# Weight strips and residual tiles moved as 120 + 8 partitions instead of eight row groups

## The chip, the cores and the metric

The kernel runs on one core of one Trainium2 chip. The metric is device time in microseconds from the start of the program to its end; lower is better. Before the change the median of three runs is 2310.73 us (2308.09 to 2316.26).

## The reference

The input x has 2048 tokens of 576 features. Two kinds of layer alternate, A, B, A, B, each with a residual and a layer norm in front.

```python
x = x + A(layernorm(x), wqkv, wo)          # same weights in both A layers
x = x + B(layernorm(x), mem0, Wq, Wk, Wv, Wo)
x = x + A(layernorm(x), wqkv, wo)
x = x + B(layernorm(x), mem0, Wq, Wk, Wv, Wo)

def A(x):      # 32 heads of 18, window of 8 keys at distances 0, 2, .. 14
    q, k, v = split(x @ wqkv)               # wqkv: 576 x 1728
    attn = softmax(q . k[s - 2w] * scale)   # w = 0..7, masked below 0
    return (attn . v[s - 2w]) @ wo          # wo: 576 x 576

def B(x):      # 32 heads of 128, segments of 32 tokens, 8 memory rows
    mem = mem0
    for s in range(64):
        h = concat(mem, x[32 * s : 32 * s + 32])
        o = attention(h @ Wq, h @ Wk, h @ Wv, mask) @ Wo
        mem = o[:8]                         # goes into the next segment
        out[s] = o[8:]
```

B is a recurrence: a segment's memory comes out of the segment before it.

## The kernel before

Everything is held transposed, features on partitions: 576 features are five blocks of up to 128 partitions. B's weights stay in on-chip memory for the whole run. A's weights do not fit beside them and are streamed.

The four layers run at the same time. Step t of the main loop (`b_step`) handles segment t of the first B layer (lane 0) and segment t-5 of the second (lane 1) in one set of matmuls, so there are 69 steps. An A tile has 64 tokens (`T`); there are 32 tiles in each A layer, and `a_tile(1, j)` runs ahead of lane 0, `a_tile(3, j)` between lane 0 and lane 1. One step of B has a pass for q and k (L834, L837), one for v (L881), scores (L921 to L931), the product with v (L972) and the output projection (L996). An A tile has its q, k and v projections (L572), logits (L621), the spreading of the softmax weights (L646) and its output projection (L682).

What sets the order: the kernel builds a list of operations with an engine, an estimated duration, a priority, dependencies and buffers. A planner in the program (`_Plan.run`) plays this list through at build time and emits the instructions in the order in which its own clock starts them. Each engine then executes its instructions in that fixed order. SP issues nearly all DMAs, also in order; a DMA that has to wait holds up those behind it.

A's weights are cut into 12 strips: three for each of q, k and v, and three for the output projection. A strip has 256 columns (128 for the third one of q, k and v, and of the output projection), five row blocks side by side: 1280 (or 640) bfloat16 numbers on each of 128 partitions, 320 KB or 160 KB. `wload` brings one strip for one A tile:

- the first use gathers it from the weight in HBM into a piece of `wo`'s buffer (L505, L506);
- the second and third use (`COPY = 2`) gather it into one of three `ring` buffers; after the third, L515 writes it to a copy of its own in HBM, `strips[i]`, laid out as the buffer is;
- every later use fetches this copy into a ring buffer (L509). That is 732 fetches: 488 of 320 KB and 244 of 160 KB.

A fetch into a ring buffer waits until TensorE has read the strip that was there (three strips earlier), and until that strip's own DMA had landed.

The residual of a tile, `xT` (128 x 5 x 64 float32, 160 KB), is written to `x1T` or `x3T` in HBM once A's output is added (L691), and read back by `residual` for the B lane that adds to it (L717): 32 times each for two layers, 128 transfers.

All these HBM copies have one shape. The 128 rows of a buffer lie in eight groups (`NQU`) of 16 (`RQU`), each group followed by one unused row, so that the groups are not contiguous and the outermost dimension of a transfer is 8:

```python
self.x1T = dp.tile([NQU, P // NQU + 1, NT, 5, T], F32, name="x1T")
self.strips = [dp.tile([NQU, P // NQU + 1, 5 * 256], BF16, name=f"strip{i}") for i in range(12)]
dma(out=w.t[:, 0:5 * n], in_=self.strips[i][:, 0:RQU, 0:5 * n])
```

Of the kernel before, what the change touches and what calls it, by code (L numbers as in the profile page):

```python
# [8 lines left out]
F32 = mybir.dt.float32  # L9
BF16 = mybir.dt.bfloat16  # L10
# [6 lines left out]
P = 128  # L17
# [10 lines left out]
T = 64  # L28
# [7 lines left out]
EPS = 1e-5  # L36
NQ = T // 16
CB = (0, 126, 252, 378, 448)
NQU = 8
RQU = P // NQU  # L40


class _Buf:
# [206 lines left out]
class _K:  # L250
# [37 lines left out]
    def setup(self):  # L288
        nc, tc = self.nc, self.tc
# [2 lines left out]
                                                           act_func_set_id=6, ins=[], outs=[]))  # L292
        dp = self.pool("dram", 1, space=bass.MemoryType.DRAM)
        NT = self.NT
        self.x1T = dp.tile([NQU, P // NQU + 1, NT, 5, T], F32, name="x1T")
        self.x3T = dp.tile([NQU, P // NQU + 1, NT, 5, T], F32, name="x3T")
        self.strips = [dp.tile([NQU, P // NQU + 1, 5 * 256], BF16, name=f"strip{i}") for i in range(12)]
        self.pre()

        self.ident = ident = cp.tile([P, P], BF16, name="ident")  # L300
# [190 lines left out]
    def wload(self, i, src, rows, col0, n, prio, dep):  # L491

        pl, dma = self.pl, self.nc.sync.dma_start
        step, last = rows
        self.strip_n[i] = k = self.strip_n.get(i, -1) + 1
        w = pl.buf("ring") if k else None

        def view():  # L500
            return (w.t if k else self.wo[:, i * 1280:(i + 1) * 1280])[:, 0:5 * n].rearrange("p (k n) -> p k n", k=5)

        def gather(e):
            f, v, r, m = src[0:1, col0:col0 + 1], view(), min(P, src.shape[0] - last), min(n, src.shape[1] - col0)
            dma(out=v[:, 0:4, 0:m], in_=bass.AP(f.tensor, f.offset, [[src.shape[1], P], [step * src.shape[1], 4], [1, m]]))  # L505
            (dma if k else self.nc.scalar.dma_start)(out=v[0:r, 4, 0:m], in_=src[last:last + r, col0:col0 + m])  # L506

        def fetch(e):
            dma(out=w.t[:, 0:5 * n], in_=self.strips[i][:, 0:RQU, 0:5 * n])  # L509
        if k == 0:  # L510
            o = self.first = pl.op("SP", 0.65, gather, -20.0 + 0.01 * i, lat=4.0)
            return view, (), o
        o = pl.op("SP", 0.9 if k <= COPY else 0.5, gather if k <= COPY else fetch, prio, [dep, self.strip_in.get(i)], acq=[w], lat=4.0)
        if k == COPY:
            self.strip_in[i] = pl.op("SP", 0.5, lambda e: dma(out=self.strips[i][:, 0:RQU, 0:5 * n], in_=w.t[:, 0:5 * n]), prio, [o], uses=[w])  # L515
        return view, (w,), o

    def a_tile(self, layer, j, dep, due, span):

        nc, pl = self.nc, self.pl  # L520
# [3 lines left out]
        def pr(f):  # L524
            return due - span * (1.0 - f)
        Q = PR[f"A{layer}"]
        if layer == 1:
            xT = pl.buf("x1")
# [8 lines left out]
            b = pl.op("PE", 0.16, tr, pr(0.04), [a], acq=[ps, xT], uses=[x0], mm=5)  # L537
            o_x = pl.op(AD_, _evac(320), lambda e, ps=ps: self.copy(e, xT.t[:], ps.t[:, 0:5 * T].rearrange("p (c t) -> p c t", c=5)),
                        pr(0.05), [b], uses=[ps, xT])
        else:  # L540
            xT = self.acc[0][j][0]
# [19 lines left out]
        for part in (0, 1, 2):  # L561
            ps = pl.buf("r")
            o = o_n
            for c in range(5):
                if c % 2 == 0:
                    n = 256 if c < 4 else P
                    view, w, ow = self.wload(part * 3 + c // 2, self.A_wqkv, (P, 512), part * D + CB[c], n, pr(Q[1]) - PR[f"ring{layer}"], wgate)
                w0 = c % 2 * CB[1]

                def mm(e, c=c, view=view, ps=ps, w0=w0):  # L570
                    for kc in range(5):
                        nc.tensor.matmul(ps.t[:, c * T:(c + 1) * T], lhsT=view()[:, kc, w0:w0 + P], rhs=xn.t[:, kc, :],  # L572
                                         start=(kc == 0), stop=(kc == 4))
                o = pl.op("PE", 0.146, mm, pr(Q[1] + 0.03 * part), [o, ow], acq=[ps, dst[part]] if c == 0 else (),
                          uses=[xn, *w] if c == 0 else [xn, *w, ps], lat=0.0 if c < 4 else None, mm=5)
                if c == 0 and part > 0:
                    def hcopy(e, part=part):
# [3 lines left out]
                        else:  # L581
                            self.copy(e, h, hin[0].t[:, part - 1])
                    got[part, "h"] = pl.op("DVE" if first else ("POOL", "ACT") if early else "POOL", 0.25, hcopy, pr(Q[1]), [o] if first else [o, hin[1]],
                                           uses=[dst[part]] if first else [dst[part], hin[0]])
# [22 lines left out]
        o = None  # L607
        for n, (c0, nb) in enumerate(((0, 2), (2, 2), (4, 1))):
            def prod(e, c0=c0, nb=nb):
                self.tt(e, big.t[:, c0:c0 + nb], qT.t[:, c0:c0 + nb].unsqueeze(2).to_broadcast([P, nb, AW, T]),  # L610
                        win(kT.t, c0, nb), ALU.mult)
            o = pl.op(("POOL", "DVE") if early else "POOL", (1.0 * nb + 0.05, 0.15 + 0.3 * nb), prod, pr(Q[2] + 0.02 * n), [o] if o else [got[0], got[1], got[1, "h"]],
                      acq=[big] if n == 0 else (), uses=[qT, kT] if n == 0 else [big, qT, kT], lk=True)
# [9 lines left out]
        o = o_l = pl.op("PE", 0.29, logits, pr(Q[3]), [o], acq=[psL, e_], uses=[big], mode="C", mm=20)  # L623

        def amax(e):
            v = psL.t[:, 0:P].rearrange("p (w t) -> p w t", w=AW)
            if first:
# [3 lines left out]
        o = pl.op("DVE", 0.6, amax, pr(Q[3]), [o], acq=[nmx], uses=[psL])  # L631
        o = pl.op("ACT", 0.28, lambda e: nc.scalar.activation(out=e_.t[:], in_=psL.t[:, 0:P].rearrange("p (w t) -> p w t", w=AW),
                                                              func=ACT.Exp), pr(Q[3]), [o], uses=[psL, e_])

        def norm(e):
            nc.vector.tensor_reduce(out=ssum.t[:], in_=e_.t[:].rearrange("p w t -> p t w"), axis=AX.X, op=ALU.add)
            nc.vector.reciprocal(out=ssum.t[:], in_=ssum.t[:])
        o = pl.op("DVE", 0.68, norm, pr(Q[3]), [o], acq=[ssum], uses=[e_])
        o = pl.op("DVE", 0.3, lambda e: self.tt(e, e_.t[:], e_.t[:], ssum.t[:].unsqueeze(1).to_broadcast([P, AW, 16]), ALU.mult),
                  pr(Q[3]), [o], uses=[e_, ssum], lk=True)  # L640

        def spread(ps, c0, nb):
            for c in range(nb):
                for g in range(NQ):
                    q4 = slice(g * AH, (g + 1) * AH)
                    nc.tensor.matmul(ps[g].t[:, c * P:(c + 1) * P], lhsT=self.epadT[q4, c0 + c, :],  # L646
                                     rhs=e_.t[q4].rearrange("p w t -> p (w t)"), start=True, stop=True, skip_group_check=True)
        b = o
        evs = {}
        for n, (c0, nb) in enumerate(((0, 2), (2, 3))):  # L650
            ps = [pl.buf("r") for _ in range(NQ)]
            b = pl.op("PE", 0.03 + 0.05 * nb, lambda e, ps=ps, c0=c0, nb=nb: spread(ps, c0, nb), pr(Q[4] + 0.02 * n), [b], acq=ps,
                      uses=[e_], mode="R", mm=4 * nb)
# [6 lines left out]
        for c0, nb in ((0, 2), (2, 2), (4, 1)):  # L660
# [6 lines left out]
        o = pl.op(PD, (2.6, 0.85), lambda e: self.tt(e, big.t[:, :, 0:4], big.t[:, :, 0:4], big.t[:, :, 4:8], ALU.add),  # L667
                  pr(Q[5] + 0.02), mus, uses=[big], lk=True)
        o = pl.op(PD, (1.44, 0.5), lambda e: self.tt(e, big.t[:, :, 0:2], big.t[:, :, 0:2], big.t[:, :, 2:4], ALU.add),
                  pr(Q[5] + 0.04), [o], uses=[big], lk=True)  # L670
        o = o_o = pl.op(PD, (0.78, 0.33), lambda e: self.tt(e, oT.t[:], big.t[:, :, 0], big.t[:, :, 1], ALU.add),
                        pr(Q[5] + 0.06), [o], acq=[oT], uses=[big], lk=True)
        ps = pl.buf("r")
        for mb in range(5):
            if mb % 2 == 0:
                n = 256 if mb < 4 else P
                view, w, ow = self.wload(9 + mb // 2, self.A_wo, (CB[1], CB[4]), mb * P, n, pr(Q[6]) - PR[f"ring{layer}"], o_l)
            w0 = mb % 2 * P

            def mm(e, mb=mb, view=view, ps=ps, w0=w0):  # L680
                for c in range(5):
                    nc.tensor.matmul(ps.t[:, mb * T:(mb + 1) * T], lhsT=view()[:, c, w0:w0 + P], rhs=oT.t[:, c, :], start=(c == 0), stop=(c == 4))  # L682
            o = pl.op("PE", 0.147, mm, pr(Q[6]), [o, ow], acq=[ps] if mb == 0 else (),
                      uses=[oT, *w] if mb == 0 else [oT, *w, ps], lat=0.0 if mb < 4 else None, mm=5)
        if layer == 1 and first:
            for d in self.wo_in:
                pl.after(d, o)
        o = pl.op("DVE", 0.49, lambda e: nc.vector.tensor_tensor(out=xT.t[:], in0=xT.t[:],
                                                                 in1=ps.t[:, 0:5 * T].rearrange("p (c t) -> p c t", c=5), op=ALU.add),
                  pr(Q[6]), [o], uses=[ps, xT])  # L690
        xst = pl.op("SP", 0.5, lambda e: nc.sync.dma_start(out=(self.x1T if layer == 1 else self.x3T)[:, 0:RQU, j], in_=xT.t[:]),  # L691
                    pr(0.95), [o], uses=[xT])
        (self.x1_stored if layer == 1 else self.x3_stored)[j] = xst
        xnb = pl.buf(f"xnb{layer}")
# [1 line left out]
        def wr2(e, m, rstd):  # L696
# [5 lines left out]
            for o, i, bc in views:  # L702
                self.tt(e, o, i, bc(m), ALU.subtract)
                self.tt(e, o, o, bc(rstd), ALU.mult)
        o = self.layernorm(xT, o, pr(Q[7]), wr2, 2.5, wacq=[xnb], early=early)
        o = pl.op("ACT", 0.27, lambda e: self.copy(e, xnb.t[64:128, :, 5, :], xnb.t[0:64, :, 4, :]),
                  pr(Q[7]), [o], uses=[xnb])
# [3 lines left out]
    def residual(self, lane, j, dep, prio):  # L711

        nc, pl = self.nc, self.pl
        b = pl.buf(("x3", "x5")[lane])
        xb = pl.buf("fin") if lane == 1 else None
        src = (self.x1T, self.x3T)[lane]
        o = pl.op("SP", 0.5, lambda e: nc.sync.dma_start(out=b.t[:], in_=src[:, 0:RQU, j]), prio,  # L717
                  [dep, (self.x1_stored, self.x3_stored)[lane][j]], acq=[b] if xb is None else [b, xb])
        self.acc[lane][j] = (b, o, xb)

# [443 lines left out]
```

## Time and profile before

| | |
|---|---|
| median of three runs | 2310.73 us |
| profiled execution: device time | 2308.09 us |
| profiled execution: span of the trace | 2306.4 us |
| mean granted TensorE clock | 0.977 |
| ring<-strip, L509 | 732 issues, median 574 ns each on SP |
| strip<-ring, L515 | 12 issues, median 622 ns |
| x1T<-x and x3T<-x, L691 | 64 issues, median 597 and 608 ns |
| x<-x1T and x<-x3T, L717 | 64 issues, median 575 and 574 ns |
| all DMA instructions on SP | 997 |
| DMA traffic | 265.12 MB, mean 115 GB/s |
| queue q1 (transfers issued by SP) | 145040 packets, 237.35 MB, 32.4% of 16 engines' span |
| queue q8 (instructions) | 474 packets, 7.77 MB, 1.4% of 16 engines' span |

How to read it. The span is cut by engine; PE is TensorE's matmul row and PEld its weight-load row, both fed by one sequencer. SPq is SP's queue: there, time is spent in issuing a DMA and in waiting for what it needs, and the transfer itself runs on the 16 DMA engines. "a <- b" in a table of waits means that a stood idle until b was done. "issue" is idle time for which the profile shows no wait. In lines of the stretches ("windows") the numbers after the engines' busy times are the granted clock, the mean busy share of the 16 DMA engines, and GB/s. The prediction below shows the lines of the page that it uses.

### The profile page before, as it was taken

What the parts mean: (1) busy time and instruction counts of PE and PEld (TensorE: products, weight loads), DVE (VectorE), ACT (ScalarE), POOL (GpSimd) and SP (SyncE); (2) the same over time, 40 slices, a digit from 0 to 9 for tenths busy, and PEclk for the clock granted to TensorE, in tenths of its full rate; (3) what the DMA queues carried; (4) which work ended last, traced back from release to release, by engine and by line L of the source; (5) the groups of instructions that cost most, each with busy time, mean ns of one, the idle gap of its engine ahead of it and who ended that gap; (6) DMA issues with size and microseconds to landing.
All of it is one profiled execution on the core that took longest, in us unless ns stands there. A gap on an engine that the chain in (4) does not pass through costs nothing.

```text
span 2306.4 us, 132983 instructions
## 1 busy us (share of the span) xinstructions
PE 2068.6 (90%) x60717; PEld 1754.8 (76%) x60717; DVE 1421.1 (62%) x3754; ACT 1140.4 (49%) x2803; POOL 834.1 (36%) x1289
## 2 busy tenths in 40 slices
PE   2788899999999999999999999899899899999988
PEld 1566787788778877887787888778788777877876
DVE  4466666666566666666666666566666566665565
ACT  1343544555455544555555555455455455555544
POOL 3234334433333443343344433333443333442221
PEclk7798999999999999999999999999999999999999
DMA  9643333333333333333333333333433333332220
GB/s 317 181 132 121 100 108 121 114 112 113 114 111 111 117 122 104 115 119 118 107 108 131 113 112 106 114 110 109 127 113 113 103 117 117 108 118 70 70 68 12
DMA packets 151331, 265.12 MB, mean 115 GB/s; under 512 B 16488, under 2 KB 82928, under 8 KB 150640
## 3 DMA queue, kind: packets, MB, share of 16 engines
q1 hardware_dynamic: 145040, 237.35, 32.4%
q0 software_dynamic: 4576, 18.88, 2.4%
q8 instruction: 474, 7.77, 1.4%
q14 instruction: 89, 0.73, 0.1%
q10 hardware_dynamic: 1152, 0.39, 0.1%
HBM read 240.46 MB, written 16.12 MB: 111 GB/s over the span
## 4 chain that ended last, share of the span: by engine, by line
PE 59%; DMA 36%; issue 2%; DVE 1%; SPq 1%; ACT 0%; ACTq 0%; DVEq 0%
DMA ring<-strip 33%; PE r L834 19%; PE r L996 15%; PE r L881 7%; PE r L837 4%; PE r L572 4%; PE r L682 2%; PE r L972 2%; PE r L646 1%; DMA x<-in_B_mem_dram 1%; PE r L931 1%; PE r L472 1%; PE r L921 1%; DMA ring<-in_A_wqkv_dram 1%; PE r L621 1%
## 5 line engine op out<-in xcount | busy, mean ns | idle before, releaser
L834 PE MATMUL r<-hT,wq 128*128 128x80 bf16 (+1 forms) x8832 | 664.4, 199 | 6.2 <-issue 2.9
L834 PE MATMUL r<-hT,wk 128*128 128x80 bf16 (+1 forms) x8832 | 665.6, 199 | 1.9 <-issue 1.9
L834 PEld LDWEIGHTS <-wq 128*128 128x128 bf16 x8832 | 504.5, 99 | 49.4 <-issue 36.9
L837 PE MATMUL r<-hT,wqk_r 128*128 128x160 bf16 (+1 forms) x2208 | 509.1, 231 | 0.0
L278 ACT ACTIVATE qk<-r 128x480 bf16<-128x480 f32 (+2 forms) x668 | 351.0, 526 | 276.8 <-PE r L837 265.7
L834 PEld LDWEIGHTS <-wk 128*128 128x128 bf16 x8832 | 449.8, 100 | 3.4 <-issue 3.3
L996 PE MATMUL r<-OT,wo 128*128 128x80 bf16 (+1 forms) x11040 | 419.7, 201 | 26.1 <-issue 21.8
L996 PEld LDWEIGHTS <-wo 128*128 128x128 bf16 x11040 | 397.8, 100 | 36.0 <-issue 32.1
L881 PE MATMUL r<-wv,hT 128*32 128x512 bf16 x5376 | 360.4, 385 | 1.5 <-issue 1.2
L285 POOL TENSOR_TENSOR big<-qT,kT 128x1024 bf16<-128x1024 bf16 x189 | 314.5, 1684 | 122.1 <-ACT kT L278 83.3
L285 POOL TENSOR_TENSOR ex<-ex,sum 128x320 bf16<-128x320 bf16 x138 | 107.1, 776 | 580.1 <-DVE sum L781 540.8
L572 PE MATMUL r<-xn,ring 128*128 128x64 bf16 x4725 | 207.9, 195 | 107.0 <-DMA ring<-strip 83.9
L572 PEld LDWEIGHTS <-ring 128*128 128x128 bf16 x4725 | 167.8, 99 | 147.7 <-DMA ring<-strip 109.1
L881 PEld LDWEIGHTS <-hT 128*32 128x32 bf16 x6720 | 172.4, 97 | 132.1 <-issue 9.7
L278 ACT ACTIVATE V<-r 128x512 bf16<-128x512 f32 x305 | 181.6, 596 | 181.2 <-PE r L881 181.0
L770 DVE TENSOR_REDUCE nmx<-r 128x8 f32<-128x320 f32 x276 | 133.4, 483 | 160.7 <-PE r L925 160.0
L837 PEld LDWEIGHTS <-wqk_r 128*128 128x128 bf16 x2208 | 220.6, 100 | 0.0
L278 ACT ACTIVATE OT<-r 128x320 bf16<-128x320 f32 (+1 forms) x378 | 134.4, 422 | 159.0 <-PE r L972 158.0
L278 ACT ACTIVATE big<-r 128x256 bf16<-128x256 f32 (+1 forms) x288 | 109.3, 430 | 88.7 <-PE r L646 87.9
L285 POOL TENSOR_TENSOR xnb<-x,st 128x256 bf16<-128x256 f32 x124 | 64.5, 520 | 235.9 <-DVE st L478 235.9
L771 DVE TENSOR_TENSOR r<-r,nmx 128x320 f32<-128x320 f32 x276 | 137.8, 499 | 9.5
L1015 DVE CAST hT<-r 128x64 bf16<-128x64 f32 (+1 forms) x68 | 14.9, 220 | 197.2 <-PE r L996 197.1
(147 smaller groups left out, 2989.8 us busy)
## 6 DMA issues: line engine op xcount, KB each, us to landing
ring<-strip SPq DMA_DIRECT2D x488, 320.0 KB
ring<-strip SPq DMA_DIRECT2D x244, 160.0 KB
x1T<-x SPq DMA_DIRECT2D x32, 160.0 KB
x<-x1T SPq DMA_DIRECT2D x32, 160.0 KB
x3T<-x SPq DMA_DIRECT2D x32, 160.0 KB
x<-x3T SPq DMA_DIRECT2D x32, 160.0 KB
wo<-in_B_Wo_dram POOLq DMA_DIRECT2D x4, 1152.0 KB, 25.3
wq<-in_B_Wq_dram POOLq DMA_DIRECT2D x2, 2048.0 KB, 21.2
```

Of the source, the lines that this page charges most:

```text
L278: nc.scalar.activation(out=out, in_=in_, func=ACT.Copy, scale=1.0 if scale is None else scale)
L285: (self.nc.vector if e == "DVE" else self.nc.gpsimd).tensor_tensor(out=out, in0=in0, in1=in1, op=op)
L472: nc.tensor.matmul(psf, lhsT=(self.ones if c < 4 else self.ones_h)[:, :], rhs=xs.t[:, c].rearrange("p a t -> p (a t)"), start=(c == 0), st ...
L572: nc.tensor.matmul(ps.t[:, c * T:(c + 1) * T], lhsT=view()[:, kc, w0:w0 + P], rhs=xn.t[:, kc, :], start=(kc == 0), stop=(kc == 4))
L682: nc.tensor.matmul(ps.t[:, mb * T:(mb + 1) * T], lhsT=view()[:, c, w0:w0 + P], rhs=oT.t[:, c, :], start=(c == 0), stop=(c == 4))
L770: nc.vector.tensor_reduce(out=m, in_=v, axis=AX.X, op=ALU.max, negate=True)
L771: nc.vector.tensor_tensor(out=v, in0=v, in1=m.unsqueeze(len(shp) - 1).to_broadcast(shp), op=ALU.add)
L834: nc.tensor.matmul(pv[:, hh, wi, a:b], lhsT=self.Wb[wi][0][:, kc, h * P:(h + 1) * P], rhs=hT.t[:, kc, a:b], start=(hh == 0 and wi == 0 and ...
L837: nc.tensor.matmul(pv[:, hh, :, a:b], lhsT=self.Wb[0][1][:, h * P:(h + 1) * P], rhs=hT.t[:, 4:6, a:b], start=False, stop=(hh == n - 1), sk ...
L881: nc.tensor.matmul(ps.t[c * 32:(c + 1) * 32, :], lhsT=l, rhs=w, start=(kc == 0), stop=(kc == 4))
L972: nc.tensor.matmul(ps[c].t[:, i * n + a - c0:i * n + z - c0], lhsT=V[b].t[q4, r, i, :], rhs=pt.t[q4, i, b, a:z], start=(i == 0 and b == bl ...
L996: nc.tensor.matmul(psY.t[:, mb * W80 + c0:mb * W80 + c1], lhsT=self.wo[:, w0:w0 + P], rhs=self.OT[:, h % 16 // 4 * 8 + h // 16 * 4 + h % 4 ...
```

## The change

The HBM copies lose their groups and unused rows: they are plain tensors of 128 rows. Each transfer to or from them is issued as two DMAs, one for partitions 0 to 119 and one for partitions 120 to 127. The planner's costs, dependencies, buffers and priorities are as before: both DMAs belong to one planned operation, so they stand next to each other in SP's order, and the instruction that uses the data waits for both.

```diff
-NQU = 8
-RQU = P // NQU
+PQU = (slice(0, 120), slice(120, 128))
...
-        self.x1T = dp.tile([NQU, P // NQU + 1, NT, 5, T], F32, name="x1T")
-        self.x3T = dp.tile([NQU, P // NQU + 1, NT, 5, T], F32, name="x3T")
-        self.strips = [dp.tile([NQU, P // NQU + 1, 5 * 256], BF16, name=f"strip{i}") for i in range(12)]
+        self.x1T = dp.tile([P, NT, 5, T], F32, name="x1T")
+        self.x3T = dp.tile([P, NT, 5, T], F32, name="x3T")
+        self.strips = [dp.tile([P, 5 * 256], BF16, name=f"strip{i}") for i in range(12)]
...
         def fetch(e):
-            dma(out=w.t[:, 0:5 * n], in_=self.strips[i][:, 0:RQU, 0:5 * n])
+            for p in PQU:
+                dma(out=w.t[p, 0:5 * n], in_=self.strips[i][p, 0:5 * n])
...
         if k == COPY:
-            self.strip_in[i] = pl.op("SP", 0.5, lambda e: dma(out=self.strips[i][:, 0:RQU, 0:5 * n], in_=w.t[:, 0:5 * n]), prio, [o], uses=[w])
+            self.strip_in[i] = pl.op("SP", 0.5, lambda e: [dma(out=self.strips[i][p, 0:5 * n], in_=w.t[p, 0:5 * n]) for p in PQU], prio, [o], uses=[w])
...
-        xst = pl.op("SP", 0.5, lambda e: nc.sync.dma_start(out=(self.x1T if layer == 1 else self.x3T)[:, 0:RQU, j], in_=xT.t[:]),
+        xst = pl.op("SP", 0.5, lambda e: [nc.sync.dma_start(out=(self.x1T if layer == 1 else self.x3T)[p, j], in_=xT.t[p]) for p in PQU],
...
-        o = pl.op("SP", 0.5, lambda e: nc.sync.dma_start(out=b.t[:], in_=src[:, 0:RQU, j]), prio,
+        o = pl.op("SP", 0.5, lambda e: [nc.sync.dma_start(out=b.t[p], in_=src[p, j]) for p in PQU], prio,
```

## The prediction, made before the changed kernel was run

> **What bounds the kernel now.** I read the page's busy shares first, then its chain of waits, then the table of who waited for whom, then one burst of transfers in the chain and in SP's timeline, then the share of the DMA engines in short windows.
>
> ```profile
> PE 2068.6 (90%) x60717; PEld 1754.8 (76%) x60717; DVE 1421.1 (62%) x3754; ACT 1140.4 (49%) x2803; POOL 834.1 (36%) x1289
> ...
> PE 59%; DMA 36%; issue 2%; DVE 1%; SPq 1%; ACT 0%; ACTq 0%; DVEq 0%
> ```
>
> TensorE is the busy engine, and what the chain holds besides it is DMA; ACT, DVE and POOL hardly appear. Another line of the chain gives 33% to "ring<-strip", the fetches of A's weight strips (line 509). The table of waits says what that costs, over the whole span:
>
> ```profile
> PE r L572 <- DMA ring<-strip: 83.9, 158, 2.8
> PE r L682 <- DMA ring<-strip: 31.2, 33, 1.8
> ...
> PEld L572 <- DMA ring<-strip: 109.1, 171, 3.3
> PEld L834 <- issue: 40.2, 84, 2.9
> PEld L682 <- DMA ring<-strip: 35.2, 33, 1.9
> ```
>
> The columns are us in total, times, longest. The matmul row idles 115.1 us for strips, the weight-load row 144.3 us. I take the second as the loss: a matmul after a stall counts as busy for its whole 193 ns, though in a running stream the next one starts 36 ns later (the chain gives eight L834 matmuls 0.29 us). The mean stall is 0.64 us at L572 and 1.07 us at L682. From 300 to 2250 us, the same table shows no wait of TensorE for DVE, ACT or POOL over 1 us, and under 13 us of them in sum.
>
> Why the strips are late:
>
> ```profile
> 1010.47 5.88 DMA ring<-strip
> 1016.35 0.05 issue
> 1016.40 0.32 PE r L572 x5
> ```
>
> ```profile
> 1009.10 1.94 SPq L509 DMA_DIRECT2D ring<-strip  x3
> 1011.09 0.64 SPq L691 DMA_DIRECT2D x3T<-x  x1
> ```
>
> ```profile
> 1011.00:1013.00 2.00, 2.00 (x50) 1.85 (x46) 1.87 (x7) 1.81 (x4) 0.00 (x0) 1.00 0.49 173
> 1013.00:1015.00 2.00, 2.00 (x55) 2.00 (x53) 1.83 (x7) 1.25 (x5) 0.23 (x1) 1.00 0.47 161
> 20.00:40.00 20.00, 5.41 (x100) 4.75 (x99) 3.65 (x13) 2.24 (x8) 1.83 (x2) 0.78 1.04 386
> ```
>
> SP issues three strips from 1009.10 on, one per 0.66 us (0.574 us each plus its semaphores); the third, issued at 1010.47, lands at 1016.35, 7.25 us after the burst began, and TensorE waits for it. The last two columns of the windows are the share of the 16 DMA engines and GB/s. While the burst is in flight the share is stuck at 0.47 to 0.49, although in the weight load at 20 to 40 us it reaches 1.04 and 386 GB/s: a strip runs on about half of the engines.
>
> **What the Trainium skill says.** "DMA: Bandwidth & Descriptors", section "Why a DMA increments its semaphore by 16 and not by 1": a transfer uses the largest number k of engines up to 16 that divides the slowest dimension of both sides, the lowest-numbered k for SP. Eight row groups against 128 partitions give 8, which agrees with the 0.47 to 0.49. The same rule gives 15 for 120 partitions and 8 for 8; no run here shows those yet. The same page, "Rules for kernel authors", says not to split a transfer into partition halves, as both serialize on the same engines. That assumes each half would use all 16 alone; here the one transfer uses 8. "Runtime: NRT & Kernel Launch", section "Instruction fetch mechanics": an engine's instructions arrive by its own DMA queue in blocks of 16 KiB. The page's q8 has 474 packets and 7.77 MB, 16.4 KB each, which agrees.
>
> **The change, part by part.** Instruction order on PE, DVE, ACT and POOL stays, as no cost or dependency of the planner is touched; on SP each transfer concerned becomes two neighbours.
>
> *Transfer, shorter.* A 320 KB strip on 8 engines is 16 rows of 2560 B on each, 40,960 B. At 173 GB/s over 0.49x16 = 7.8 engines, an engine moves 22 GB/s, so 1.86 us; a burst of 320+320+160 KB takes 4.65 us. Of the 7.25 us, the first issue's 0.57 and some 2.0 us of fixed latency remain. With 15 engines a strip is 8 rows each (0.93 us), plus one row on eight of them.
>
> *Issue, doubled.* 0.57 us is what every transfer with k = 8 takes, 160 or 320 KB. The trace has no k = 15 issue: a gather on 128 partitions (L505) shows 0.37 at the least, an x store 0.60. I take 0.6 for each, with semaphores 1.25 us a pair; bounds 0.8 and 2.0.
>
> *Sum for a burst, from its first issue.* First strip: before 0.57+2.0+1.86 = 4.4; after, main part 0.57+2.0+0.93 = 3.5, tail earlier. Saved 0.9. Second: before 0.57+2.0+2x1.86 = 6.3; after 1.25+0.57+2.0+0.93 = 4.75. Saved 1.5. Third: before 7.25; after, the tail's issue ends at 3.75, plus 2.0: 5.75. Saved 1.5. From here SP's issue sets the pace, not the transfers.
>
> *Stalls.* With 0.9 to 1.5 us less against mean stalls of 0.64 and 1.07 us, most vanish and the long ones (up to 3.3) are cut: I take 85% of 144.3 = 123 us; bounds 80 (70% of the 115.1) and 144.
>
> *Given back.* A stall also covers other things: TensorE's instruction blocks (idle for "issue" on PEld lines: 40.2 at L834, 34.1 at L572, 32.1 at L996, 20.3 at L972) catch up during it, and the chains through ACT, DVE and POOL have had that time. They are on time now, but nothing shows by how much. I take a quarter, 31 us; bounds a tenth and a half.
>
> *Edits at little or nothing.* TensorE must await two semaphores per strip, so 732 more semaphore instructions at 51 ns (the 60 at L572 now); they run ahead in the sequencer, hidden under matmuls in flight; uncovered, 37 us. The 128 stores and residual loads of x (L691, L717) add 0.6 us each to SP, 77 us in all, hidden in SP's idle time (997 issues at 0.57 are a quarter of its span); uncovered only where a strip stands behind them, and then inside the strip's 0.9 us saving. The 12 strip writes (L515) add 7 us to SP at 88 to 132 us, where TensorE does wait for gathers: I take +3, bounds 0 and 7.
>
> Sum against the profiled execution (span 2306.4, its time 2308.1, 2.6 below the median 2310.7): -123 + 31 + 3 = -89 us. On the median: 2222 us; own range 2180 (144 gone, a tenth back) to 2271 (80 gone, half back).
>
> **Rivals.**
> *The gain is hidden (13%).* The stalls go, and the instruction blocks or the softmax chain of B become late instead. For: 174 us of "issue" idle on PEld already. Against: it would need to eat over 100 of 123 us, where no ACT or DVE wait shows now. Time: 2310.7 - 13 = about 2297.
> *Instruction blocks share an engine with strips: slower (11%).* Place: q8, 474 blocks, 1.4% of 16 engines, so 1.1 us each. If its engine is among those that carry strips only after the change, a block queues behind rows: 220 MB (732 fetches and the 128 transfers of x) on 15 engines, at the 20 GB/s per busy engine that q1 shows over the span (237.35 MB in 32.4% of 16 engines), keep each busy for 730 us, 32% of the span, so 152 blocks meet rows and wait up to a whole share, 0.93 us: 141 us. Decides from 89/152 = 0.6 us per block met. Time: 2222+141 = 2363 at the worst, 2345 taken. For: TensorE starves for instructions at times already. Against: a row of 2560 B is gone after 0.12 us at 22 GB/s, and the DMA page, section "Queues, rings and completion order", says queues take turns by packets; one row's wait gives 18 us. And k = 15 leaves engine 15 free.
> *SP's issue is dear: slower (6%).* If a pair takes over (7.25-2.0)/3 = 1.75 us, the third strip lands later than before. At 2.0 it is 0.75 us later, in some 150 stalls, with the first two a little sooner: about +60, 2370. Against: no issue of such a shape takes over 0.62 us at the median.
> That k stays 8 for the 120 rows (then doubled issue for nothing) is in that last case.
>
> **How the numbers follow.** Likeliest case 70%: 2222. Changes within 0.3% (7 us) cannot be told from none. Faster: 69 of the 70, 7 of the 13, 2 of the others: 0.78; same 0.07; slower 0.15. The range reaches from 2180 up through the hidden case, to 2312.
>
> **What would show it.** DMA share in bursts near 0.7 or above instead of 0.48, and waits of PEld for ring<-strip under 40 us in sum; third strips of a burst under 6 us after its first issue; SP issues of 0.5 to 0.7 us, two per strip. Wrong if issues take over 0.9, if "issue" idle on PEld grows by over 90 us, or if q8's share rises clearly over 1.4%.

## The result, and the profile after

The changed kernel takes 2204.53 us (median of four runs, 2200.21 to 2209.72); the kernel before, run beside it, 2311.47 us. The ratio is 0.9537, with a 95% interval of 0.9506 to 0.9567. The profiled execution has a span of 2206.2 us against 2306.4.

The busy shares and the chain of waits of the changed kernel, from its page:

```profile
PE 2041.7 (93%) x60717; PEld 1741.3 (79%) x60717; DVE 1417.7 (64%) x3754; ACT 1139.6 (52%) x2803; POOL 835.1 (38%) x1289
...
q1 hardware_dynamic: 158120, 237.40, 39.0%
...
q8 instruction: 477, 7.82, 1.6%
...
PE 83%; DMA 10%; issue 4%; DVE 1%; SPq 1%; ACT 1%; POOL 0%; ACTq 0%; DVEq 0%; POOLq 0%
```

DMA fell from 36% of the chain to 10%, and TensorE's own work rose from 59% to 83%. "issue" doubled, from 2% to 4%.

One line of the table of waits before the change, and then the table of the changed kernel (us in total, times, longest):

```profile
PE r L996 <- issue: 21.8, 25, 3.1
```

```profile
PE r L996 <- issue: 44.3, 54, 2.2
...
PE r L572 <- DMA ring<-strip: 14.0, 22, 2.0
...
PE r L682 <- DMA ring<-strip: 3.3, 9, 0.6
```

```profile
PEld L996 <- issue: 61.3, 73, 2.3
...
PEld L572 <- issue: 36.2, 56, 9.3
...
PEld L572 <- DMA ring<-strip: 11.6, 19, 2.0
...
PEld L682 <- DMA ring<-strip: 3.9, 8, 0.7
```

The weight-load row waited 144.3 us for strips before and waits 15.5 us now. Its idle time for "issue", summed over all lines, went from 178.6 to 222.5 us (the 174 us of the prediction are its eight largest lines); the largest growth is at L996, from 32.1 to 61.3. L996 uses no strip. On the matmul row the waits for strips went from 115.1 to 17.3 us, and "issue" from 40.6 to 70.2.

One burst of three strips in the changed kernel, from SP's timeline and from two stretches of the DMA engines (last columns: granted clock, share of 16 engines, GB/s):

```profile
960.34 2.16 SPq L509 DMA_DIRECT2D ring<-strip  x6
962.59 0.67 SPq L691 DMA_DIRECT2D x3T<-x  x2
```

```profile
961.00:963.00 2.00, 2.00 (x81) 1.31 (x68) 1.93 (x5) 1.48 (x4) 0.00 (x0) 1.00 0.74 207
963.00:965.00 2.00, 2.00 (x54) 2.00 (x52) 1.77 (x8) 1.22 (x3) 0.00 (x0) 1.00 0.97 238
```

Six issues take 2.16 us, hardly more than three did before (1.94). The share of the DMA engines reaches 0.97, where a burst was held to 0.47 to 0.49 before; the rate rises less, from 161 and 173 GB/s to 238.

### The profile page after: what moved, and what is told of

It reads as the page before. It is cut to its first block, busy times and chain, and to the rows that moved or that the text cites. A ratio compares the mean times of both kernels' runs of the same rounds, so it can differ in the third digit from the quotient of the medians.

```text
span 2206.2 us, 134717 instructions
## 1 busy us (share of the span) xinstructions
PE 2041.7 (93%) x60717; PEld 1741.3 (79%) x60717; DVE 1417.7 (64%) x3754; ACT 1139.6 (52%) x2803; POOL 835.1 (38%) x1289
## 4 chain that ended last, share of the span: by engine, by line
PE 83%; DMA 10%; issue 4%; DVE 1%; SPq 1%; ACT 1%; POOL 0%; ACTq 0%; DVEq 0%; POOLq 0%
PE r L834 27%; PE r L996 17%; PE r L881 15%; DMA ring<-strip 7%; PE r L572 6%; PE r L837 6%; PE r L972 3%; PE r L682 2%; PE r L646 1%; PE r L471 1%; PE r L931 1%; PE r L921 1%; DMA ring<-in_A_wqkv_dram 1%; DMA x<-in_B_mem_dram 1%; PE r L621 1%
## 5 line engine op out<-in xcount | busy, mean ns | idle before, releaser
L996 PE MATMUL r<-OT,wo 128*128 128x80 bf16 (+1 forms) x11040 | 421.1, 200 | 50.8 <-issue 44.3
L996 PEld LDWEIGHTS <-wo 128*128 128x128 bf16 x11040 | 396.3, 100 | 65.0 <-issue 61.3
L572 PE MATMUL r<-xn,ring 128*128 128x64 bf16 x4725 | 185.8, 194 | 34.1 <-DMA ring<-in_A_wqkv_dram 14.2
L572 PEld LDWEIGHTS <-ring 128*128 128x128 bf16 x4725 | 161.5, 98 | 57.8 <-issue 26.9
```

Of the source, the lines that this page charges most:

```text
L996: nc.tensor.matmul(psY.t[:, mb * W80 + c0:mb * W80 + c1], lhsT=self.wo[:, w0:w0 + P], rhs=self.OT[:, h % 16 // 4 * 8 + h // 16 * 4 + h % 4 ...
```

## The experiments

Ten kernels were run. Each ratio is to the kernel before on the same chip, whose median was 2311 to 2329 us, so ratios and not times are to be compared. Waits are of the weight-load row of the profiled execution, in us; "issue" is summed over all lines.

| kernel | median us | ratio (95%) | waits for strips | "issue" | q1, share of 16 engines |
|---|---|---|---|---|---|
| before | 2311.47 to 2329.44 | 1 | 144.3 | 178.6 | 32.4% |
| changed | 2204.53 | 0.9537 (0.9506 to 0.9567) | 15.5 | 222.5 | 39.0% |
| e1: one DMA, 128 plain rows | 2148.76 | 0.9231 (0.9189 to 0.9274) | 6.7 | 185.0 | 35.8% |
| e2: 120 + 8, both on 8 engines | 2390.47 | 1.0281 (1.0235 to 1.0327) | 188.7 | 203.9 | 31.5% |
| e3: strips alone | 2209.76 | 0.9500 (0.9459 to 0.9541) | 25.8 | 220.5 | 39.0% |
| e4: last 8 rows alone | 2087.49 | 0.8971 (0.8938 to 0.9004) | 0 | 136.6 | 9.5% |
| e5: sixteen groups | 2215.97 | 0.9536 (0.9511 to 0.9561) | 35.5 | 213.9 | 40.3% |
| e6: four groups | 2878.79 | 1.2387 (1.2336 to 1.2438) | 571.0 | 197.6 | 23.0% |
| e7: 64 + 64 | 2228.58 | 0.9592 (0.9562 to 0.9622) | 28.9 | 228.3 | 38.8% |
| e8: 120 rows alone | 2196.58 | 0.9450 (0.9421 to 0.9480) | 11.7 | 225.9 | 37.4% |
| e9: one DMA, padded rows | 2148.86 | 0.9240 (0.9193 to 0.9287) | 7.0 | 173.6 | 35.9% |
| e10: residual tiles alone | 2336.97 | 1.0040 (1.0019 to 1.0062) | 168.3 | 182.1 | 33.3% |

**e2: the same two DMAs, on eight engines.** My theory was that the number of engines carries the gain; the rival, that splitting does.

```diff
+PQU = ((slice(0, 120), slice(0, 15)), (slice(120, 128), slice(15, 16)))
...
-            dma(out=w.t[:, 0:5 * n], in_=self.strips[i][:, 0:RQU, 0:5 * n])
+            for p, g in PQU:
+                dma(out=w.t[p, 0:5 * n], in_=self.strips[i][:, g, 0:5 * n])
```

> The same two DMAs of 120 and 8 partitions, but the HBM copies stay in eight groups with gaps, so that both run on 8 engines. If the number of engines is the cause, nothing is gained: a burst is still 4.65 us of transfer, waits of PEld for strips stay at 130 to 190 us, and the doubled issue costs a little: 2305 to 2345 us, ratio 0.998 to 1.015. If the gain came from splitting itself (two completions, smaller pieces) rather than from the engines, the time is near the changed kernel's, ratio 0.95 to 0.97.

The ratio is 1.0281. Splitting in this shape gains nothing: it loses 2.8%, more than I had allowed. The weight-load row waits 44 us longer for strips, which is inside the expected band, and 25 us longer for "issue". Not only the number of engines tells this kernel from the changed one: SP's issue of a piece of a strip has a median of 654 ns here and of 316 ns there. The next two runs change the number of engines with far less change in the issue.

**e6 and e5: four groups, sixteen groups.** One constant of the kernel before is changed, and nothing else.

```diff
-NQU = 8
+NQU = 4
```

> The kernel before with four row groups of 32: four engines by the rule, so 102,400 B per engine become 204,800 in a burst, 9.3 us at 22 GB/s, and the third strip lands 0.57 + 2.0 + 9.3 = 11.9 us after the first issue instead of 7.25. If the engines' number sets the flight, DMA share in the steady part stays below 0.25, waits of PEld for strips rise from 144 to over 900 us, and the time is 2950 to 3600 us. If flight is mostly latency that the number of engines does not touch, the time is below 2600 us.

The waits with four groups, and one steady stretch:

```profile
PEld L572 <- DMA ring<-strip: 460.0, 308, 7.0
PEld L682 <- DMA ring<-strip: 111.0, 72, 3.7
```

```profile
1000.00:1200.00 200.00, 161.02 (x4204) 134.35 (x4201) 97.33 (x255) 77.38 (x189) 61.82 (x96) 0.90 0.25 90
```

The direction and the resource are as expected: the mean share of the DMA engines over 200 us stands at 0.25, four of sixteen. The size is a miss: 571 us of waits and 2879 us, where I had expected over 900 and at least 2950. Nor are the waits all of the loss. The span grew by 573 us, the matmul row's waits for strips by 406; its busy time grew by 206 us, at a granted clock of 0.90 in this stretch against 0.99 in the same stretch before.

> The kernel before with one constant changed: sixteen row groups of 8 with gaps instead of eight of 16; one DMA per transfer, on 16 engines by the rule. If the number of engines alone is the cause, the time is that of the single DMA of 128 plain rows, ratio to before 0.918 to 0.930. If the gaps cost by themselves (SP's issue took 0.574 us with groups and 0.32 without), SP's issue stays above 0.5 us and the ratio is 0.935 to 0.955.

Sixteen groups give 0.9536, the second of the two outcomes, and SP's issue stays at a median of 543 ns. With four, eight and sixteen groups the issue is much the same (507, 574 and 543 ns), so these two runs show the number of engines as the cause: sixteen instead of eight is worth 4.6% even with the groups. The groups lose a further three points to plain rows:

**e1 and e9: one DMA of 128 rows.**

```diff
-PQU = (slice(0, 120), slice(120, 128))
+PQU = (slice(0, 128),)
```

> The HBM copies are plain tensors of 128 rows, as in the changed kernel, but each transfer is one DMA of 128 partitions. If the number of engines is what counts and the second issue is only a cost, a burst lands sooner still (0.57 + 2.0 + 2.3 = 4.9 us for the third strip, against 5.75): waits of PEld for strips below 10 us, 2185 to 2204 us, ratio to before 0.945 to 0.954. If it matters that the sixteenth engine stays free of strips (instruction blocks on it), idle for "issue" on PEld rises by 20 us or more over the changed kernel's 222, and the time is 2215 us or more.

It is faster than both kernels: 0.9231, further than either case allowed, with 6.7 us of waits for strips. A strip of 320 KB lands at a median of 3.5 us after its issue began, with sixteen groups 4.2. The lines of the page, plain rows first, then sixteen groups:

```profile
q1 hardware_dynamic: 152016, 237.38, 35.8%
...
ring<-strip SPq DMA_DIRECT2D x488, 320.0 KB, 3.5
```

```profile
q1 hardware_dynamic: 152016, 237.38, 40.3%
...
ring<-strip SPq DMA_DIRECT2D x488, 320.0 KB, 4.2
```

Both move the same bytes in the same number of packets. But 40.3% of 16 engines over 2213.4 us is 93.9 ns per packet, and 35.8% over 2146.7 us is 80.9 ns. The same sum gives 87.1 ns for the changed kernel and 82.4 ns for the kernel before. Plain rows also have less "issue" idle (185.0) than the changed kernel (222.5), though their strips are on sixteen engines.

> As the single DMA of 128 plain rows, but each row of a strip's copy in HBM is 128 bytes longer than what is moved, so that the rows do not touch. If the sixteen groups lost 3% against the plain rows because their rows are not one contiguous block, the ratio rises to 0.94 to 0.955 here too. If it is the shape of the access (groups by rows, three dimensions) that costs, in SP's issue and in the spread over engines, it stays at 0.918 to 0.930, with SP's issue at 0.3 to 0.4 us.

With rows that do not touch, the time is that of e1 (0.9240) and SP's issue has a median of 382 ns in both. So contiguous memory is not what plain rows have over groups. What is left is the shape of the access; how much of it acts through SP's issue and how much through the time per packet was not separated.

**e7 and e8: what the changed kernel loses against one DMA.**

```diff
-PQU = (slice(0, 120), slice(120, 128))
+PQU = (slice(0, 64), slice(64, 128))
```

> Plain rows, two DMAs per transfer of 64 partitions each, so 16 engines for both. It has the changed kernel's number of issues and completions, and the single DMA's number of engines. If the second issue and completion cost the 58 us between the changed kernel and the single DMA, the ratio is 0.945 to 0.960. If it is the uneven spread of 120 + 8 over 15 and 8 engines, the ratio is 0.920 to 0.932.

```diff
-            for p in PQU:
+            for p in PQU[:1]:
```

> As the changed kernel, but a strip's fetch leaves out partitions 120 to 127, which keep what the buffer held. One DMA on 15 engines. If the second DMA is what costs against the single one of 128, the ratio is 0.915 to 0.930, like that one's. If 15 engines are slower in themselves, it is 0.940 to 0.955.

64 + 64 gives 0.9592, 3.6 points behind one DMA. This does not price the second DMA of the changed kernel, because SP's issue of 64 rows is dear. One DMA of 128 first, then 64 + 64 (least, median and longest, in ns):

```profile
L509 SPq DMA_DIRECT2D ring<-strip x732: 319/382/2297, 136.8 to 2062.5; - x183
```

```profile
L509 SPq DMA_DIRECT2D ring<-strip x1464: 444/587/2056, 136.1 to 2141.5; - x183
```

The strips come late for it, and the table above hides how late: the matmul row waits 68.1 us for them, the weight-load row 28.9.

```profile
PE r L572 <- DMA ring<-strip: 51.4, 67, 4.4
```

120 rows alone give 0.9450, between the changed kernel (0.9537) and one DMA of 128 (0.9231), although 6% of a strip's bytes are not moved. So a strip's second DMA, with its rows, costs the changed kernel about 0.9 points. The other 2.2 points are not slower strips. Counted in the traces, over bursts of three strips that stand alone on SP for 8 us, the strips' last packet ends 4.9 us after the first issue in e8 and in e1 alike (medians). What differs is the matmul row's idle time for "issue", 79.8 us in e8 and 45.5 in e1: 34 of the 49 us between the two spans. A further part can be the residual tiles, which e8 still splits and e1 does not (e10, below). Why TensorE has more of this idle time with fifteen engines than with sixteen was not settled.

**e3 and e10: the two parts of the change.** The edits undo the change for the residual tiles (e3) or for the strips (e10).

> Only the strips are split in 120 and 8; the residual tiles stay in eight groups with one DMA each. By my theory the gain is the strips': 2200 to 2215 us, ratio 0.952 to 0.958; SP saves 128 issues, 77 us of its own time, which nothing waits for. If the residual tiles carry a real part of it (their stores and loads stand in front of strips on SP and on the same engines), the time is 2225 us or more.

> Only the residual tiles are split in 120 and 8; the strips stay in eight groups with one DMA each. The strips alone gave 0.950, the whole change 0.954, so nothing should be left for the tiles: ratio 0.99 to 1.01, waits of PEld for strips at 125 to 150 us. If both parts overlap in what they gain, this one alone gives 0.96 to 0.985.

The strips alone give 0.9500, the whole change 0.9537; the tiles alone 1.0040. The gain is the strips'. The tiles' split gains nothing and may cost some 0.4%. One expectation missed: with the tiles alone the weight-load row waits 168.3 us for strips, not 125 to 150. The profiled execution was one of the slowest of its kernel (2352.84 us, median 2336.97), so part of this may be its own.

**e4: what is left when strips cost nothing.**

```diff
-            for p in PQU:
+            for p in PQU[1:]:
```

> As the changed kernel, but a strip's fetch brings only partitions 120 to 127; the other 120 keep what the buffer held, so that nearly no bytes move and one issue per fetch is left. It shows what is left when strips cost nothing. If the idle time for "issue" on PEld (179 us before, 222 after the change) grew because TensorE runs faster, it stays at 210 to 240 us here and the time is 2175 to 2200 us. If it grew because instruction blocks meet strips on an engine, it falls back to 180 or less and the time is 2130 to 2170 us.

TensorE's waits for "issue" on the matmul row, all four lines that the table has, and q8 with q1 from the page:

```profile
PE r L996 <- issue: 1.3, 3, 0.7
PE r L931 <- issue: 0.8, 2, 0.5
PE r L834 <- issue: 0.7, 2, 0.4
PE r L881 <- issue: 0.6, 1, 0.6
```

```profile
q1 hardware_dynamic: 59300, 49.97, 9.5%
...
q8 instruction: 474, 7.77, 1.6%
```

The time falls to 0.8971, further than either case allowed. The matmul row's "issue" idle is 3.4 us, against 40.6 before the change and 70.2 after it, and the weight-load row's is 136.6 against 178.6 and 222.5. (So most of the weight-load row's "issue" idle costs nothing: 136.6 us of it are there when the matmul row has 3.4.) TensorE runs faster here than in any other run, so its speed alone does not starve it; without the strips' traffic it is not starved. L996 shows it best: its "issue" idle of 61.3 us on the weight-load row in the changed kernel is 8.2 us here.

That this idle time is a wait for instruction blocks can be counted in the traces. The 477 blocks of q8 in the changed kernel fit TensorE's 122,176 instructions at 256 to a block. From 300 to 1900 us TensorE stands still 71 times for over 0.3 us; 58 of these, 50.8 of 57.3 us, end at an instruction whose number in TensorE's order leaves the same remainder on division by 256, and each of them ends 1.2 to 1.7 us after a packet of q8 has ended. In e1 it is 44 stalls of 46; in e4 there is no stall of this length.

Traffic alone does not make blocks late, though. With four groups (e6) the same 237 MB move, and the matmul row has two lines of "issue", 1.8 us in sum:

```profile
PE r L996 <- issue: 1.0, 3, 0.4
PE r L834 <- issue: 0.8, 4, 0.3
```

In e6 the strips are on four engines only, TensorE waits 521 us for strips, in which blocks can catch up, and its clock is lower. No run separates these three.

## Why the prediction was right

The forecast was 2222 us, 89 us less than before; measured were 107 us between the medians and 100 us between the profiled executions.

**What bounds it, and the number of engines.** Right. The rule of the Trainium skill, "DMA: Bandwidth & Descriptors", section "Why a DMA increments its semaphore by 16 and not by 1", agrees with the runs: the share is 0.25 with four groups, 0.47 to 0.49 in a burst with eight, 0.97 with 120 + 8. The share cannot tell fifteen engines from sixteen (15/16 is 0.94, and the measure reads 1.04 in the weight load). The packets can: counted in the traces from 300 to 1900 us, the number of q1 packets in flight that lasts longest (none apart) is 4 in e6, 8 before, 15 in the changed kernel and in e8, and 16 in e1, e5 and e9; only in 64 + 64 it is unclear, 14 with 13 and 15 close by. The time follows it, 1.239, 1 and 0.954 for 4, 8 and 16 groups.

**The sum for a burst.** The saving was forecast well, from two terms mis-sized in opposite directions, which is partly luck. In bursts of three strips that stand alone on SP for 8 us, the strips' last packet ends 6.9 us after the first issue before the change (median of 24) and 5.4 us after it (median of 38): 1.4 us less, where 1.5 was forecast for the third strip. But the issue was taken at 0.6 us with bounds from the kernel before; it has a median of 316 ns, and six take 0.36 us each with all around them instead of 0.62. Groups had made it dear: sixteen groups still take 543 ns where 128 plain rows take 382. They are not the only thing that does, as the 587 ns of 64 + 64 show. The transfer was taken at 22 GB/s per engine, as with eight; at a share of 0.97, 15.5 engines moved 238 GB/s, 15.3 GB/s each. So transfers still set the pace of a burst, and not SP, as the step had it: the six issues are over after 2.2 us at the median, the packets after 5.4. In the chain, a tail that TensorE waited for looks like this:

```profile
969.90 4.96 DMA ring<-strip
...
975.00 0.31 PE r L572 x5
```

The fetch issued at 969.90 took 4.96 us to land. Its burst began at 967.08, so the last piece came 7.8 us later, no sooner than the 7.25 us of the burst before the change; one issue in it had taken 1.25 us. Such bursts are the exception that is left. In most nothing waits any more, which is why this kind of piece is 7% of the chain and not 33%.

One effect is not in the sum: a fetch waits until the DMA that filled its buffer before has landed, so shorter flights can let later fetches start sooner. SP's waits of this kind at L509 fell from 495.5 to 156.6 us; what that was worth was not separated.

**Stalls.** Right: 123 us forecast, 144.3 - 15.5 = 128.8 measured on the weight-load row.

**Given back.** The size was near, 31 us against 29.6 on the matmul row and 43.9 on the weight-load row. The quarter had nothing behind it, as the prediction says itself, so this is luck. The reason was incomplete. I expected instruction blocks to be late because the stalls in which they caught up are gone. In e4 the stalls are gone too, and the blocks are on time; it takes the strips' traffic besides. This was so before the change as well: 178.6 - 136.6 = 42 us of the old kernel's "issue" idle on the weight-load row is not there in e4. That long stalls hide late blocks is not refuted; e6, with the longest, has the least of them on the matmul row. ACT, DVE and POOL took next to nothing back: from 300 us on the matmul row waited 1.4 us for them before and 3.3 after.

**The sum.** On the matmul row it closes. Idle time fell by 73.3 us: strips -97.8, "issue" +29.6, all other waits -5.6, to within 0.5 us. Busy time fell by 26.9 us, of which 25.1 are at the two lines that read strips, L572 and L682 (L682 from 66.8 to 63.8). L572 before and after:

```profile
L572 PE MATMUL r<-xn,ring 128*128 128x64 bf16 x4725 | 207.9, 195 | 107.0 <-DMA ring<-strip 83.9
```

```profile
L572 PE MATMUL r<-xn,ring 128*128 128x64 bf16 x4725 | 185.8, 194 | 34.1 <-DMA ring<-in_A_wqkv_dram 14.2
```

Together that is the 100.2 us of the span, and it bears out why the prediction took the weight-load row for the loss: a stall costs the matmul row its wait and some busy time after it, 97.8 + 25.1 = 122.9 us here. The 11 us by which the forecast was short are small terms: the other waits, the 3 us allowed for strip writes, which are not seen (waits of the weight-load row for gathers of wqkv at L572 are 15.0 and 15.2 us), and the rest of the busy time. The mean granted clock rose from 0.977 to 0.989, most of it in the first 170 us (0.82 and 0.93); it is no large part of the gain, as the busy time of the lines without strips fell by only 1.8 us.

**Edits at little or nothing.** Right for the two semaphores per strip: 550 semaphore instructions at L572 where there were 60, 51 ns each, and L572 has 36.2 us of "issue" idle on the weight-load row after 34.1 before. They are hidden as supposed: of TensorE's 739 semaphore instructions, 706 ran while a matmul was in flight. About right for the tiles' stores and loads, which gain nothing and may cost 0.4%. A second DMA per strip was not free: about 0.9 points by e8, and 2.8 and 3.6 in the shapes of e2 and e7, where an issue takes about twice as long.

**The rivals.** "The gain is hidden" did not happen. "Instruction blocks share an engine with strips" named a real cost, at a third of the 141 us named. Its mechanism is neither shown nor refuted: with sixteen plain rows strips are on sixteen engines and the idle time is 185, less than with fifteen, while with four engines the matmul row hardly has any; no run shows on which engine q8 is. The argument against it took one row of 2560 B for the packet by which queues take turns, which the section that it names does not state. "SP's issue is dear" failed at 0.36 us per issue. The advice of the Trainium skill against two partial transfers ("DMA: Bandwidth & Descriptors", section "Rules for kernel authors") agrees with e7 against e1, where one DMA already has sixteen engines; it does not speak of a transfer that has eight.

**The signs.** The share, the waits for strips and the burst came as named. The issue did not: 0.316 us and not 0.5 to 0.7. q8's share rose from 1.4 to 1.6%, which was named as a sign of being wrong, but it means little: e4, with hardly any strips and no late blocks, has 1.6% too.

## What to carry to other kernels

Look at the share of the DMA engines while transfers are in flight. Here a burst that stopped at half of them, with TensorE waiting at its end, was one whose shape gave it half of the engines. Try the plain shape first, one DMA with all 128 partitions as its outermost dimension; here that took 7.7% off, where a split into 120 + 8 took 4.6%. Traffic that nothing waits for can still cost through late instructions, so count "issue" idle on the matmul row next to the waits for data.

## What the runs showed of the hardware

SP's time to issue one DMA of a strip depends on the shape; the medians are 574 ns with eight groups, 543 with sixteen, 507 with four, 382 for 128 plain rows, 358 for 120 and 263 for 8 of them, but 587 for each of 64 + 64. What makes 64 rows dearer than 128 is open.

TensorE's wait for its own instructions varies with DMA traffic and its shape: 3.4 us of idle time on the matmul row with 50 MB on q1, and with 237 MB 1.8 us on four engines, 40.6 on eight, 45.5 in plain rows on sixteen, 73.8 in sixteen groups, 70.2 with 120 + 8. Fetching a block did not take much longer: q8's share of 1.2 to 1.6% is 1.1 to 1.2 us per block throughout. What delays the blocks is open; no run separated it.
